# Second-layer products moved behind the branches of a mixture-of-experts kernel, with two loads and two gathers in another order

## The chip, the cores and the metric

The kernel runs on one core of one Trainium2 chip. The metric is the time of one execution on the device, in microseconds (us). It has five engines that matter here: TensorE (PE, with PEld for its weight loads and a sequencer that reads its instructions), VectorE (DVE), ScalarE (ACT), GpSimd (POOL) and SyncE (SP).

## What is computed

Attention within chunks of 64 positions, and then a layer of eight experts of which each row takes one:

```python
def _attn_ref(q, k, v) -> np.ndarray:
    ...
    scores = scale * np.matmul(q_c, k_c.transpose(0, 1, 2, 4, 3))
    scores = scores - np.max(scores, axis=-1, keepdims=True)
    attn = np.exp(scores)
    attn = attn / (np.sum(attn, axis=-1, keepdims=True) + 1e-09)
    out = np.matmul(attn, v_c)
...
    logits = x @ w_gate
    expert_idx = np.argmax(logits, axis=1)
...
    for e in range(E):
        mask = expert_idx == e
        ...
        xe = x[mask]
        h = np.maximum(xe @ w1[e], 0.0)
        ye = h @ w2[e]
        out[mask] = gate_w[mask, None] * ye
```

There are 4608 rows of 512 numbers, each expert's first layer is 512 x 1024 and its second 1024 x 512, all in float32.

## The kernel before, in words

**Slots.** The first 120 us or so compute attention and the gate and sort the rows by expert in DRAM. The rest, which the change touches, runs in slots: one slot is 256 rows of one expert and, where that saves a slot of its own, 64, 128 or 192 extra rows of the same expert. How many extra rows a slot has is known only on the device (`kind`: 0, 1, 2, 3), so each slot has four forms behind branches (L1323 to L1325): `form_a` without extra rows, and `form_x` with 64, 128 or 192. Behind the branches comes the common part of the slot, and then the branch into the next slot's form. With these inputs slots 0 to 15 run, slot 0 still among the work on attention. Slot 1 has 64 extra rows, slots 5 and 7 as well, slot 9 and slot 12 have 192, slot 10 has 128, and the others none.

**Products.** Each float32 product is made of three products of split operands: high by high, low by high and high by low. The high part of weights and of hidden values is written by ScalarE (L82, L710), the low part by VectorE (L83, L715). A slot goes through eight blocks f of 128 hidden columns. For each, the first layer fills one bank (L683 in the plain form, L690 with extra rows), the ReLU writes high and low part, and two blocks later `block(f)` adds the second layer's products to bank U (rows 0 to 127, m = 0) and bank V (rows 128 to 255, m = 1), three matmuls each (L776 to L778). Extra rows have banks K and Q and go through `more(f)`.

**The end of a slot.** Before the change a form ends with blocks 4 and 5 for both banks, twelve products, and for extra rows with their finishes (L801 to L803, L807) and the stores of their results (L808; tile y2 for the first 128 or 64 extra rows, y3 for the next 64). The common part then splits the next rows (L663, L664; in slot 1 TensorE transposes them, L634), splits chunks 4 and 5 of the next weights (L82, L83), adds blocks 6 and 7 in bank U, and finishes bank U on ScalarE (L805). [...]

**Weights.** An expert's weights are sixteen chunks, high and low, for two sets in turn. They arrive in four raw tiles of two chunks each: raw0 for chunks 0 and 1, raw1 for 2 and 3, raw2 for 4 and 5, raw3 for 6 and 7. A split is one instruction on ScalarE and one on VectorE. `split_step(u, i)` splits one chunk behind block i and issues the load that can go as soon as a raw tile is free.

**Queues.** All indirect transfers go through GpSimd in the order of the code: the loads of weights (L581), the gathers of rows (L608: xg3 and xg5 for extra rows of the next slot, xg4 twice for the rows of the slot after it) and the stores (L808). Each counts on one of eight semaphores (DMASW0 to DMASW7), which the framework hands out in turn; in a form without a certain store an instruction on GpSimd adds what the store would have added. Who waits for a transfer in the common part waits for the semaphore's value there, and that includes every transfer counted on it before.

**Code.** `PLACE` and `addr_align` (in the 192-row form) set where the code of TensorE's forms stands in blocks of 256 instructions; `hint` tells TensorE's sequencer at block 4 which form comes next.

Of the kernel before, what the change touches and what calls it, by code (L numbers as in the profile page):

```python
# [40 lines left out]
XW = D + 16  # L41
HB = 3
WARM = 36
PLACE = {1: 87, 2: 110, 3: 110}
BLOCK = 256
SKEW = 128
BIG = 1.0e6
# [3 lines left out]
def attn_moe_kernel(ctx: ExitStack, tc: tile.TileContext, q, k, v, wg, w, w0, out):  # L51
# [27 lines left out]
    def split_chunk(par, c):  # L79
        hi, lo = w_hi[par][c], w_lo[par][c]  # L80
        src = raw[c // 2][:, (c % 2) * 1024:(c % 2 + 1) * 1024]
        nc.scalar.copy(hi, src)  # L82
        nc.vector.tensor_tensor(lo, src, hi.bitcast(F32), ALU.subtract)  # L83
# [20 lines left out]
    def bank(tag, shape):  # L104
        n = 1
        for x in shape[1:]:
            n *= x
        if tag == "S":
            t = psum[0].tile([P, 512], F32, name="psS", tag="S", bufs=2)
        else:  # L110
            t = slots[tag][turns[tag] % len(slots[tag])]
            turns[tag] += 1
        t = t[0:shape[0], 0:n]
        if len(shape) == 3:
            t = t.rearrange("p (a b) -> p a b", b=shape[2])
        return t
# [459 lines left out]
    def wset(u):  # L576

        return 0 if u < 2 else (u + 1) % 2

    def load_w(u, c):  # L580
        nc.gpsimd.indirect_dma_start(  # L581
            out=raw[c][:, :], out_offset=None,
            in_=w, in_offset=bass.IndirectOffsetOnAxis(ap=widx[:, u, c:c + 1], axis=0),
            bounds_check=4 * E * P - 1, oob_is_err=False)
# [21 lines left out]
    def rows_in(t, u, h):  # L606
        rows = TE[u] * P if u < 2 and h < 2 else NT
        return nc.gpsimd.indirect_dma_start(  # L608
            out=t[:, :], out_offset=None, in_=xd[0:rows, :],
            in_offset=bass.IndirectOffsetOnAxis(ap=place(u, h)[0:t.shape[0], :], axis=0),  # L610
            bounds_check=rows - 1, oob_is_err=False)
# [6 lines left out]
    def gather_x(u):  # L618
        rows_in(xg3, u, 2)
        rows_in(xg5, u, 3)  # L620
# [25 lines left out]
    def spread(u):  # L646

        for h in range(2):
            ids(u, rows_of(u)[h], h)
        for a in range(4):  # L650
            for b in range(4):
                nc.sync.dma_start(
                    xq.rearrange("p (h a) x -> p h a x", a=4)[b * 32:(b + 1) * 32, :, a, :],
                    xg4[a * 32:(a + 1) * 32, 2:4, b * P:(b + 1) * P])
# [63 lines left out]
    def gemm1(par, f, hh=None, hl=None):  # L718
        ph = bank("X", [P, BLK]) if f % 3 == 2 else bank("S", [P, BLK])
        gemm1_pe(par, f, ph)  # L720
        return gemm1_lo(ph, relu_hi(ph, hh), hl)
# [36 lines left out]
    def rest_0():  # L758

        gemm2(0, 7, h0[7], 1, last[0])  # L760
        finish(0, 1, last[0][1])
# [8 lines left out]
    def gemm2(par, f, h, m, py):  # L770
        gemm2_pe(par, f, *(x[:, m * P:(m + 1) * P] for x in h), py[m])
# [41 lines left out]
    def split_step(u, i):  # L813

        if i < 2:
            if u < 2:
                load_w(u + 1, 2 + i)
                return
            split_chunk(wset(u), 6 + i)
            if i == 1:  # L820
                load_w(u + 1, 3)
                load_w(u + 1, 2)
        else:
            split_chunk(wset(u + 1), i - 2)
            if i % 2:
                load_w(u + 2, i // 2 - 1)

    used = [0]

# [37 lines left out]
    def find_u(u):  # L867
        return find(idx[u % 3], rowm[:, u, :], rowm[:, u, :], KB - 1) if u < NU else iter(())
# [106 lines left out]
    def slot_kinds():  # L975

        S2 = [P, NU, E]
        for h in range(2):
            ids(1, rows_of(1)[h], h)
        yield "v"  # L980
        nc.vector.tensor_tensor(o_b, iota_f[:, 0:NU].unsqueeze(2).broadcast_to(S2),
                                end.broadcast_to(S2), ALU.is_equal)
        yield "v"
        nc.vector.tensor_tensor(o_b, o_b, knd.broadcast_to(S2), ALU.mult)
        yield "v"
        with nc.allow_low_precision("whole numbers"):
            nc.vector.tensor_reduce(kind[:, 0:NU], o_b, AX.X, ALU.add)
# [233 lines left out]
    h_of = h0[5:8] + h0[5:8] + [[hq.tile([P, BLK], F32R, name=f"{x}{f}") for x in ("hh", "hl")] for f in (6, 7)]  # L1221

    def rest(u, py):

        for f in (6, 7):
            gemm2(wset(u), f, h_of[f], 1, py)
        finish(u, 1, py[1])

    def slot(u, kd, nxt, left=None):
        par = wset(u)  # L1230
        py = [bank("UV"[m], [P, D]) for m in range(2)]
        if u > 1:
            spread(u + 1)

        def block(f, h, ms=(0, 1)):
            for m in ms:
                gemm2(par, f, h, m, py)

        def later():

            if u == 1:
                yield from slot_kinds()
                yield "v"
                yield from places()
            yield from find_u(u + 3)

        def some(x, n):
            for _ in range(n):
                next(x, None)

        def form_a():
            if u == 1:
                rest_0()
            if left is not None:
                rest(u - 1, left)
            h = []
            x = later()
            for f in range(8):
                h.append(gemm1(par, f, *h_of[f]))
                if f == 4 and u + 1 < SMAX:  # L1260

                    hint(u + 1, kind_of(u + 1, PE) if u == 1 else nxt)
                if f == 0 and u > 1:
                    gather_x(u + 1)
                if f == 5 and u > 1:
                    turn()
                    gather(u + 2)
                if f < 7:
                    if f < 6:
                        split_step(u, f)  # L1270
                    some(x, 5 if u == 1 else 1)
                if 1 < f < 6:
                    block(f - 2, h[f - 2])
            assert next(x, 0) == 0
            for f in (4, 5):
                block(f, h[f])

        def form_x(n):

            make_xt_x(u, n)  # L1280
            if u == 1:
                rest_0()
            if left is not None:
                rest(u - 1, left)
            pe = [bank(x, [P, D]) for x in ("K", "Q")[0:-(-n // EXT)]]

            h = []
            x = later()

            def more(f):  # L1290
                gemm2_x(par, f, h[f][1], pe)

            for f in range(8):
                h.append(gemm1_x(par, f, n, *h_of[f]))
                if f == 4 and u + 1 < SMAX:
                    hint(u + 1, kind_of(u + 1, PE) if u == 1 else nxt)
                if f == 0 and u > 1:
                    gather_x(u + 1)
                if f == 5 and u > 1:
                    turn()  # L1300
                    gather(u + 2)
                if f < 7:
                    if f < 6:
                        split_step(u, f)
                    some(x, 5 if u == 1 else 1)
                if 1 < f < 5:
                    block(f - 2, h[f - 2][0])
                if 1 < f < 7:
                    more(f - 2)
                if f == 4 and n > EXT:  # L1310
                    nc.tensor.addr_align(BLOCK, offset=PLACE[u if u == 1 else 3 if u >= SMIN - 1 else 2], max_nops=0)
            assert next(x, 0) == 0
            more(5)
            block(3, h[3][0])
            more(6)
            more(7)
            for f in (4, 5):
                block(f, h[f][0])
            for i, p in enumerate(pe):
                m = min(EXT, n - i * EXT)  # L1320
                finish(u, 2 + i, p, m)

        with tc.If(kd > 0, label=f"kind{u}") as c:  # L1323
            with tc.If(kd > 1, label=f"half{u}") as c2:
                with tc.If(kd < 3) as c3:  # L1325
                    form_x(EXT)
                with c3.Else():
                    form_x(EXW)
            with c2.Else():
                form_x(HALF)  # L1330
        with c.Else():
            form_a()

        nc.gpsimd.drain()
        if u == 1:
            make_xt(u + 1)
        else:
            make_xs()
        for c in (4, 5):
            split_chunk(wset(u + 1), c)  # L1340
        for f in (6, 7):
            block(f, h_of[f], (0,))
        finish(u, 0, py[0], on_act=True)
        if u + 1 < SMIN:
            return py
        rest(u, py)
# [54 lines left out]
```

## Time and profile before

| what | value |
|---|---|
| median of 3 runs | 570.3 us (568.74 to 572.33) |
| the profiled execution, its own time | 571.92 us |
| its span in the profile | 570.0 us, 13232 instructions |
| granted TensorE clock, mean | 0.994 of full speed |
| busy, TensorE / VectorE / ScalarE / GpSimd | 553.8 / 425.1 / 280.9 / 270.4 us |
| bytes moved | 102.70 MB, mean 180 GB/s |

A busy time is the sum of an engine's instructions, with overlaps counted once. TensorE's weight loads run beside its products. An instruction's start and duration are on the clock of the span, which begins at 0; 570.0 of the 571.92 us lie inside it. [...]

### The profile page before, as it was taken

The numbers are of one execution on the slowest core, as the hardware profiler recorded it, in microseconds if no ns is written. First come the engines' busy times: TensorE is split into PE (matmuls) and PEld (weight loads), VectorE is DVE, ScalarE is ACT, GpSimd is POOL, SyncE is SP. The second block draws the span as 40 slices with busy tenths as digits, with TensorE's granted clock in tenths as the row PEclk, the third lists the DMA queues.
The fourth block names the chain that finished last, engine by engine and source line by source line (L and its number), as shares of the span: only waits on it lengthen the run. The fifth ranks groups of instructions, "written<-read, shape, count | busy, mean of one in ns | idle before, by whom it ended". The sixth has DMA issues, their size and how long they took to land.

```text
span 570.0 us, 13232 instructions
## 1 busy us (share of the span) xinstructions
PE 553.8 (97%) x4858; PEld 488.3 (86%) x4858; DVE 425.1 (75%) x832; ACT 280.9 (49%) x542; POOL 270.4 (47%) x289
## 2 busy tenths in 40 slices
PE   5999999999999999999999999999998999999995
PEld 5888888888998888989898898888988888798894
DVE  8889999996694978776787588645666764588775
ACT  1477776662244464554555355424444542456453
POOL 6013763586643754535484575522514242275352
PEclk9899999999999999999999999999999999999998
DMA  8999999744674652456145636554622662232121
GB/s 273 399 326 347 376 340 361 269 157 184 231 257 138 185 184 61 137 188 218 44 139 174 210 93 208 163 189 147 209 72 85 205 206 67 68 104 77 22 59 39
DMA packets 49038, 102.70 MB, mean 180 GB/s; under 512 B 14176, under 2 KB 28512, under 8 KB 45312
## 3 DMA queue, kind: packets, MB, share of 16 engines
q0 software_dynamic: 19776, 61.14, 31.4%
q1 hardware_dynamic: 29120, 39.88, 21.1%
q8 instruction: 63, 1.03, 0.7%
q14 instruction: 79, 0.65, 0.4%
HBM read 113.75 MB, written 19.56 MB: 234 GB/s over the span
## 4 chain that ended last, share of the span: by engine, by line
PE 76%; issue 10%; DMA 5%; POOL 3%; DVE 2%; POOLq 1%; ACT 1%; ACTq 0%
PE psS L683 12%; PE psS L690 10%; PE psS L251 6%; DMA xg<-xd,idx 5%; PE psV L776 4%; PE psV L777 4%; PE psV L778 4%; PE psU L778 4%; PE psU L777 4%; PE psU L776 4%; PE psL L690 3%; PE psL L683 3%; PE psU L306 3%; PE psT L329 2%; PE psT L297 2%
## 5 line engine op out<-in xcount | busy, mean ns | idle before, releaser
L83 DVE TENSOR_TENSOR wlo<-raw,whi 128x1024 fp32r<-128x1024 f32 x118 | 142.3, 1216 | 16.9 <-ACT whi L82 16.3
L82 ACT CAST whi<-raw 128x1024 fp32r<-128x1024 f32 x118 | 121.9, 1046 | 2.2 <-DMA raw<-in_w,widx 2.2
L581 POOL DMA_INDIRECT raw<-in_w,widx x62 | 71.9, 1160 | 91.1 <-DVE wlo L83 62.2
L710 ACT ACTIVATE hh<-psS 128x256 fp32r<-128x256 f32 x98 | 37.7, 385 | 156.8 <-PE psS L683 79.5
L808 POOL DMA_INDIRECT out_y<-y,oid x40 | 51.9, 1299 | 110.4 <-issue 35.3
L683 PE MATMUL psS<-xhl,whi 128*128 128x256 f32 x496 | 91.8, 284 | 0.9 <-PE psV L778 0.5
L608 POOL DMA_INDIRECT xg<-xd,idx x68 | 78.7, 1157 | 26.5 <-issue 17.3
L683 PEld LDWEIGHTS psS<-xhl,whi 128*128 128x128 f32 x496 | 79.7, 191 | 5.4 <-issue 1.3
L715 DVE SCALAR_TENSOR_TENSOR hl<-psS,hh 128x256 fp32r<-128x256 f32 x98 | 41.1, 421 | 57.1 <-ACT xx L694 37.8
L683 PE MATMUL psS<-xhl,wlo 128*128 128x256 f32 x248 | 70.2, 283 | 0.0
L690 PE MATMUL psS<-xhl,whi 128*128 128x320 f32 (+2 forms) x288 | 59.8, 333 | 0.5 <-ACT xhl L674 0.5
L690 PEld LDWEIGHTS psS<-xhl,whi 128*128 128x128 f32 x288 | 49.6, 188 | 4.6 <-ACT xhl L674 0.6
L776 PE MATMUL psV<-whi,hh 128*128 128x512 f32 x128 | 51.1, 399 | 1.5 <-issue 1.5
L776 PE MATMUL psU<-whi,hh 128*128 128x512 f32 x128 | 50.4, 394 | 0.0
L777 PE MATMUL psU<-wlo,hh 128*128 128x512 f32 x128 | 50.4, 393 | 0.0
L778 PE MATMUL psU<-whi,hl 128*128 128x512 f32 x128 | 50.2, 392 | 0.0
L777 PE MATMUL psV<-wlo,hh 128*128 128x512 f32 x128 | 50.1, 391 | 0.0
L778 PE MATMUL psV<-whi,hl 128*128 128x512 f32 x128 | 50.0, 390 | 0.0
L683 PEld LDWEIGHTS psS<-xhl,wlo 128*128 128x128 f32 x248 | 47.4, 191 | 0.0
L90 POOL TENSOR_TENSOR wlo<-raw,whi 128x512 fp32r<-128x512 f32 x16 | 20.2, 1277 | 43.7 <-DMA kb<-in_k 27.3
L452 POOL DMA_INDIRECT xd<-xb,di x32 | 31.7, 989 | 18.0 <-issue 13.1
L776 PEld LDWEIGHTS psV<-whi,hh 128*128 128x128 f32 x128 | 24.0, 188 | 7.7 <-issue 2.3
(255 smaller groups left out, 1150.1 us busy)
## 6 DMA issues: line engine op xcount, KB each, us to landing
qt<-in_q SPq DMA_DIRECT2D x17, 512.0 KB
xg<-xg SPq DMA_DIRECT2D x224, 32.0 KB
vb<-in_v SPq DMA_DIRECT2D x12, 512.0 KB
kb<-in_k SPq DMA_DIRECT2D x22, 256.0 KB
raw<-in_w SPq DMA_DIRECT2D x16, 256.0 KB
spare<-in_k SPq DMA_DIRECT2D x12, 256.0 KB
spare<-in_v SPq DMA_DIRECT2D x6, 512.0 KB
xg<-xd,idx POOLq DMA_INDIRECT x68, 3.5
```

What stands on the lines that cost most here:

```text
L82: nc.scalar.copy(hi, src)
L83: nc.vector.tensor_tensor(lo, src, hi.bitcast(F32), ALU.subtract)
L581: nc.gpsimd.indirect_dma_start(out=raw[c][:, :], out_offset=None, in_=w, in_offset=bass.IndirectOffsetOnAxis(ap=widx[:, u, c:c + 1], axis= ...
L608: return nc.gpsimd.indirect_dma_start(out=t[:, :], out_offset=None, in_=xd[0:rows, :], in_offset=bass.IndirectOffsetOnAxis(ap=place(u, h)[ ...
L683: nc.tensor.matmul(ph, a, b[:, kc, 0:BLK], start=kc + i == 0, stop=kc + i == 5)
L690: nc.tensor.matmul(ph, a[par][kc][:, f * 128:(f + 1) * 128], b[:, kc, 0:BLK + n], start=kc + i == 0, stop=kc + i == 5)
L710: nc.scalar.activation(hh, ph, AF.Relu)
L715: nc.vector.scalar_tensor_tensor(hl, ph, 0.0, hh.bitcast(F32), ALU.max, ALU.subtract)
L776: nc.tensor.matmul(py, hh, wh, start=f == 0, stop=False)
L777: nc.tensor.matmul(py, hh, wl, start=False, stop=False)
L778: nc.tensor.matmul(py, hl, wh, start=False, stop=f == 7)
L808: nc.gpsimd.indirect_dma_start(out=outs[m], out_offset=bass.IndirectOffsetOnAxis(ap=oid[u % 3][0:n, m:m + 1], axis=0), in_=y, in_offset=No ...
```

## The change

Three edits, in every slot:

1. A form ends with block 4 in bank U alone. Block 4 in bank V and block 5 in both, nine products, move behind the branch into the common part, ahead of blocks 6 and 7. The code of the forms becomes shorter, and the constants of `PLACE` grow by 36.
2. `split_step` issues the load of raw2 before that of raw3.
3. The gathers for extra rows (`gather_x`) move from behind block 0 to behind the load of raw0 in the fourth `split_step`.

```diff
-PLACE = {1: 87, 2: 110, 3: 110}
+PLACE = {1: 123, 2: 146, 3: 146}
...
             if i == 1:
+                load_w(u + 1, 2)
                 load_w(u + 1, 3)
-                load_w(u + 1, 2)
         else:
             split_chunk(wset(u + 1), i - 2)
             if i % 2:
                 load_w(u + 2, i // 2 - 1)
+                if i == 3 and u > 1:
+                    gather_x(u + 1)
...
-                if f == 0 and u > 1:
-                    gather_x(u + 1)
...
-            for f in (4, 5):
-                block(f, h[f])
+            block(4, h[4], (0,))
...
-                if f == 0 and u > 1:
-                    gather_x(u + 1)
...
-            for f in (4, 5):
-                block(f, h[f][0])
+            block(4, h[4][0], (0,))
...
         for c in (4, 5):
             split_chunk(wset(u + 1), c)
+        block(4, h_of[4], (1,))
+        block(5, h_of[5])
         for f in (6, 7):
             block(f, h_of[f], (0,))
```

What that does to the engines' orders. TensorE, end of the 128-row form, before (bank U and V for block 4 with hh_2680, then for block 5 with hh_2714, then the jump to the common part):

```order
L776 MATMUL psU_88<-whi1_6_2749,hh_2680 128x512
L777 MATMUL psU_88<-wlo1_6_2757,hh_2680 128x512
L778 MATMUL psU_88<-whi1_6_2749,hl_2685 128x512
L776 MATMUL psV_89<-whi1_6_2749,hh_2680 128x512
L777 MATMUL psV_89<-wlo1_6_2757,hh_2680 128x512
L778 MATMUL psV_89<-whi1_6_2749,hl_2685 128x512
L776 MATMUL psU_88<-whi1_6_2749,hh_2714 128x512
...
L778 MATMUL psV_89<-whi1_6_2749,hl_2792 128x512
L1325 UNCONDITIONAL_BRANCH
```

and the same place now, with the last of the extra rows' products (bank K) ahead of it:

```order
L778 MATMUL psK_93<-whi1_7_2750,xx_4321 128x512
L776 MATMUL psU_88<-whi1_6_2749,hh_2680 128x512
L777 MATMUL psU_88<-wlo1_6_2757,hh_2680 128x512
L778 MATMUL psU_88<-whi1_6_2749,hl_2685 128x512
L1321 UNCONDITIONAL_BRANCH
```

The nine products between the fourth and the jump are gone from here; they follow in the common part, so that on the way through a slot their order is the old one. Only in slot 1 do the transposes of L634 come before them.

GpSimd, the part of one slot from the first extra gather to the last weight load, before (xg_65 and xg_66 are the two extra gathers, raw_2742 is raw3, raw_2741 raw2, raw_67 raw0, raw_68 raw1; ISA is the instruction that adds to a semaphore):

```order
L608 DMA xg_65<-xd,idx_285 128x528
L1397 ISA
L608 DMA xg_66<-xd,idx_285 64x528
L581 DMA raw_2742<-in_w,widx 128x2048
L581 DMA raw_2741<-in_w,widx 128x2048
L581 DMA raw_67<-in_w,widx 128x2048
L590 COMPARE_AND_BRANCH
L590 UNCONDITIONAL_BRANCH x2
L608 DMA xg_64<-xd,idx_286 128x528 x2
L581 DMA raw_68<-in_w,widx 128x2048
```

and now:

```order
L581 DMA raw_2741<-in_w,widx 128x2048
L1395 ISA
L581 DMA raw_2742<-in_w,widx 128x2048
L581 DMA raw_67<-in_w,widx 128x2048
L608 DMA xg_65<-xd,idx_285 128x528
L608 DMA xg_66<-xd,idx_285 64x528
L590 COMPARE_AND_BRANCH
L590 UNCONDITIONAL_BRANCH x2
L608 DMA xg_64<-xd,idx_286 128x528 x2
L581 DMA raw_68<-in_w,widx 128x2048
```

Raw2 has gone from the fourth place to the first, and the two extra gathers from the head of the row to behind raw0. As the semaphores are handed out in this order, others share one now.

ScalarE, common part of the same slot, before, with the semaphores that an instruction waits for:

```order
L663 CAST xhl<-y_2762 128x2x256 [waits DVE_49,PE_49]
L663 CAST xhl<-y_2762 128x2x256 [waits PE_49]
L82 CAST whi_4_73<-raw_2741 128x1024 [waits DMASW7_49]
L82 CAST whi_5_74<-raw_2741 128x1024
L805 ACTIVATE y_2762<-psU,gate_106 128x512 [waits DMASW2_49,DVE_49,PE_49]
```

and now:

```order
L663 CAST xhl<-y_2762 128x2x256 [waits DVE_49,PE_49]
L663 CAST xhl<-y_2762 128x2x256 [waits PE_49]
L82 CAST whi_4_73<-raw_2741 128x1024 [waits DMASW4_49]
L82 CAST whi_5_74<-raw_2741 128x1024
L805 ACTIVATE y_2762<-psU,gate_106 128x512 [waits DMASW2_49,DVE_49,PE_49]
```

The instructions stand as before. The split of chunk 4 waits for DMASW4 instead of DMASW7, to a value that counts raw2 and, behind it, the store of y2 at the end of the same slot's form; DMASW7 counted raw2 alone at that place.

## Rows read from the trace of the kernel before

**Rows 1.** The page, busy time of TensorE (us, share of the span, instructions).

```profile
PE 553.8 (97%) x4858; PEld 488.3 (86%) x4858; DVE 425.1 (75%) x832; ACT 280.9 (49%) x542; POOL 270.4 (47%) x289
```

**Rows 2.** Waits of TensorE, 250 to 570 us: total, times, longest.

```profile
PE psV L776 <- issue: 1.5, 1, 1.5
PE psS L683 <- PE psV L778: 0.5, 1, 0.5
```

**Rows 3.** Branches of TensorE's sequencer: ns min/median/max, start; slots 10, 10, 12, 7.

```profile
L1325 PEldq COMPARE_BRANCH  x1: 3282/3282/3282, 422.5 to 422.5; - x1
...
L1323 PEldq COMPARE_BRANCH  x1: 3208/3208/3208, 426.3 to 426.3; - x1
...
L1325 PEldq COMPARE_BRANCH  x1: 3613/3613/3613, 488.4 to 488.4; - x1
...
L1324 PEldq COMPARE_BRANCH  x1: 326/326/326, 324.6 to 324.6; - x1
```

**Rows 4.** Timeline, end of slot 10: start us, us, engine, instruction, [idle before].

```profile
421.53 0.28 DVE L697 SCALAR_TENSOR_TENSOR xx<-psS,xx 128x128 fp32r<-128x128 f32 x1
...
422.48 0.39 PE L776 MATMUL psK<-whi,xx 128*128 128x512 f32 x1
...
426.56 0.39 PE L776 MATMUL psU<-whi,hh 128*128 128x512 f32 x1
...
429.55 0.50 PE L776 MATMUL psV<-whi,hh 128*128 128x512 f32 x1 [1.46 <-issue]
```

**Rows 5.** Timeline of TensorE, end of slot 12 and start of slot 13.

```profile
488.39 0.39 PE L796 MATMUL psQ<-whi,xx 128*128 128x512 f32 x1
...
495.89 0.36 PE L683 MATMUL psS<-xhl,whi 128*128 128x256 f32 x1 [0.51 <-PE psV L778]
```

**Rows 6.** The chain of waits, 386 to 398 us, slots 9 to 10: start, us, what.

```profile
390.22 3.67 DMA out_y<-y,oid
...
396.14 1.93 PE psS L690 x11
```

**Rows 7.** Timeline of ScalarE, end of slot 9.

```profile
391.18 2.00 ACT L82 CAST whi<-raw 128x1024 fp32r<-128x1024 f32 x2
393.74 0.69 ACT L805 ACTIVATE y<-psU,gate 128x512 f32<-128x512 f32 x1 [0.56 <-PE psU L778]
394.83 0.59 ACT L674 CAST xhl<-psT 128x512 fp32r<-128x512 f32 x1 [0.40 <-PE psT L672]
```

**Rows 8.** Timeline of GpSimd, VectorE and TensorE, slots 7 to 8.

```profile
328.26 4.02 POOL L808 DMA_INDIRECT out_y<-y,oid  x1 [3.82 <-DVE y L803]
...
329.11 2.34 DVE L83 TENSOR_TENSOR wlo<-raw,whi 128x1024 fp32r<-128x1024 f32 x2
...
333.24 0.75 DVE L807 TENSOR_SCALAR y<-psV,gate 128x512 f32<-128x512 f32 x1 [1.52 <-PE psS L683]
333.91 0.41 DVE L715 SCALAR_TENSOR_TENSOR hl<-psS,hh 128x256 fp32r<-128x256 f32 x1
...
336.20 0.39 PE L778 MATMUL psU<-whi,hl 128*128 128x512 f32 x1
```

**Rows 9.** DMA queues, 332.7 to 333.3 us: packets, MB, share.

```profile
q0 software_dynamic: 48, 0.02, 14.6%
```

**Rows 10.** Timeline of VectorE and GpSimd in slot 7, a split beside a weight load.

```profile
316.81 1.23 DVE L83 TENSOR_TENSOR wlo<-raw,whi 128x1024 fp32r<-128x1024 f32 x1 [0.38 <-ACT whi L82]
316.92 1.98 POOL L581 DMA_INDIRECT raw<-in_w,widx  x1 [0.31 <-issue]
```

**Rows 11.** Timeline, slot 8's first extra gather, and its first use in slot 9.

```profile
338.65 1.56 POOL L608 DMA_INDIRECT xg<-xd,idx  x1 [0.30 <-issue]
...
352.56 0.51 PE L672 MATMUL psT<-ident,xg 128*128 128x128 f32 x3
```

**Rows 12.** Timeline, end of slot 1: VectorE and TensorE.

```profile
176.27 0.68 DVE L802 TENSOR_TENSOR y<-psK,y 64x512 f32<-64x512 f32 x1 [2.29 <-ACT y L801]
...
176.60 0.39 PE L778 MATMUL psV<-whi,hl 128*128 128x512 f32 x1
```

## The prediction

> **What bounds the kernel now.** I read the page's busy times first, then what TensorE waits for in the slots, then the branches of its sequencer, then the two ends of slots at which something is late, and last GpSimd beside VectorE.
>
> TensorE is busy for 553.8 of 570.0 us [rows 1]. From 250 us on its waits are single: 1.5 us for "issue" at L776 in bank V and 0.5 us at L683, each once [rows 2], and two smaller ones at extra rows' transposes and their first products. So whatever hides beside TensorE is free, and a change that keeps its products can win only those few us; it can lose more wherever an operand comes late.
>
> Both waits of rows 2 are jumps. The compare-and-branch that ends the 128-row form of slot 10 holds the sequencer 3.28 us from 422.5, and the next one, from the common part into the plain form, 3.21 us from 426.3 [rows 3]. At the end of the 192-row form of slot 12 it is 3.61 us; the 64-row form's jump takes 0.33 us. What the sequencer has already passed on keeps TensorE going meanwhile: the jump at 422.5 begins with the product at 422.48, and the first product behind it starts at 426.56 [rows 4], which at one product per 0.227 us is 18 products of cover, 4.1 us. One long jump fits under that. Two in a row don't: six products stand between them, and TensorE waits 1.46 us at 429.55.
>
> **The change part by part.** The order of the products on TensorE stays as it is in all slots but the first, so their time drops out. Four things are left.
>
> *The jump comes nine products earlier.* It is followed by 15 products instead of six before the next jump. In slot 10 the sequencer would reach it at 422.5 - 9 x 0.227 = 420.5, but the last extra product needs VectorE's low half, which ends at 421.53 + 0.28 = 421.81 [rows 4], so about 421.9. With 3.28 us it resumes at 425.2. What was passed on ends where product 4 of bank U ends, at 422.48 + 9 x 0.227 = 424.5: a new gap of 0.7 us there. The next jump is met after 15 products' issue, about 0.75 us later at 425.9, takes 3.2 us and lets bank V's products through at 429.0 instead of 429.55. So -0.6 us; between 0 (the new gap eats it) and -1.46 (both hidden). In slot 12 the jump moves from 488.4, by the same rule, to about 486.7 and ends at 490.3, just before the nine remaining products of cover run out at 488.39 + 9 x 0.23 = 490.46 [rows 5]; the second jump then lies under 21 products, and the first product of slot 13, at 495.89, loses its wait and a little issue: -0.66, between +0.4 and -0.7. In slot 9, whose end shows no wait for a jump, I take 0. The plain and 64-row forms have short jumps: 0.
>
> *A wait on another transfer.* Software transfers count on eight semaphores in turn. Before, the first gather for extra rows shared its semaphore with the store of the extra results (tile y2) that stands at the form's end; the next slot's transposes therefore waited for that store too. Now the load of weight chunk 4 and 5 (tile raw2) stands first in GpSimd's row and takes that place, so ScalarE's split of chunk 4 in the common part waits for y2's landing although its own data came long before. Behind it on ScalarE stand the second split, the finish of bank U (L805), the extra rows' copy (L674) and the next slot's first ReLU; behind those, VectorE and TensorE.
>
> From slot 9 to 10 the store lands at 390.22 + 3.67 = 393.89, where the two splits had begun at 391.18 [rows 6, 7]. Then 2.00 for the splits, 0.69 for the finish and 0.59 for the copy give 397.2, and TensorE wants that copy at 396.14: +1.1 us (between 0, if ScalarE's pair was late for another reason, and +1.5). From 10 to 11 and from 12 to 13 TensorE stands at the next form's jump or has two more microseconds in hand: 0.
>
> After the 64-row slots 5 and 7 it depends on when the store starts to move. In slot 7 it is issued at 328.26 and takes 4.02 us on GpSimd [rows 8]; its 48 packets run only at 332.7 to 333.3 [rows 9], just behind the 4.02 us. If that time stays, the splits start at 333.3, the pair ends at 335.3, VectorE's pair 1.2 us behind it (2.34 for two) at 336.6, then four tiny instructions, the finish of bank V (0.75) and the low half (0.41): 338.0, and TensorE wants that low half at 336.20: +1.75, twice. But GpSimd's 4.02 us looks like VectorE's doing: a weight load issued 0.11 us after a split began on VectorE took 1.98 us and ended at 318.90, which is 0.86 us after that split's end [rows 10], and 328.26 + 4.02 = 332.28 is 0.83 us after the end of the pair at 329.11 + 2.34 = 331.45. With ScalarE held, VectorE's pair is held too; the store's issue then ends 0.85 us after L664, near 330.0, its landing comes at 331.0 and the low half at 335.9, 0.3 us before it is wanted. I take 0 for both slots, since the lag of rows 10 repeats so closely, and keep +1.75 each as the upper end.
>
> [...]
>
> *Loads and gathers trade places on GpSimd.* Eight transfers are issued in a slot as before. The gathers for extra rows now come behind three loads, which wait for splits, some 8 us later by my estimate: in slot 8 the first was issued at 338.65 and its rows are wanted at 352.56 [rows 11], so 6 us are left where a store with its landing takes 3.67 [rows 6], and 0 is its price. What hides it is the rest of the slot; issued 2 us later still, it would cost what it is late. The two row gathers and raw1 behind them keep their place from the fourth split on, at most some 2.6 us later when GpSimd is busy, with over 6 us of cover. Raw2 comes earlier, which TensorE doesn't notice: 0.
>
> *Slot 1.* There the transposes of the next rows (L634) now come before the nine products, and must wait until the extra rows' banks are read out, which VectorE's instruction at 176.27 ends at 176.95. TensorE would be at the second four at about 176.6, where bank V's last product 4 stood [rows 12]: +0.35, of which a later stall of 0.2 gives some back; I take +0.2.
>
> The constants that place the code rise by 36 each, as the code in front of them shrinks, so that the forms keep their places: 0 (a long jump gone or added, 3.3 us under 4 us of cover, at the outside +1).
>
> Sum: -0.6 - 0.66 + 1.1 + 0 + 0.2 = about 0. Made against the profiled execution (571.92 us, span 570.0), that is 572.0. It lies 1.6 above the median of the runs, 570.3, so against that the forecast is 570.5 us. About 1%, 5.7 us, is what a measurement of this kernel can tell from no change.
>
> **The rivals.**
>
> *Gains only.* Every added wait is hidden and the pair of jumps closes fully: -1.46 - 0.7 = -2.2, 568.2. For it: rows 2 hold just these waits. Against it: the sum for 9 to 10, where nothing is left to hide 2.7 us of delay on ScalarE.
>
> *The late store reaches TensorE.* The time on GpSimd stays 4.02 us in slots 5 and 7 and the delay on ScalarE is not caught up: +1.75 twice and +1.1 is +4.6, less 1.2 won, 573.7. Slower by over 1% it becomes when the lag runs through the slot: held up by some 4, 4 and 3 us at the three places, all of it on TensorE, it is +11, less the 1.2: 580. It decides from the point at which the low half of a slot's first block comes more than the 1.9 us late that lie between the end of that low half, 333.91 + 0.41, and 336.20 [rows 8]. For it: one semaphore surely counts both. Against it: what rows 10 show, and a lag that VectorE's idle time between blocks makes good.
>
> *The cover isn't 18 products.* If the sequencer runs ahead as far as it likes, the jump's place matters little. [...] As a mechanism here: with deeper cover the jump at 422.5 would have been met earlier already, so moving it would bring nothing and the nine products less of cover behind it cost 0.7 to 1.4 in slots 10 and 12, giving 573.5 with the wait of slot 9.
>
> *No visible effect for another reason.* TensorE's order is the same, so if the semaphore's wait falls early too, everything is 0: 570.3. It is part of the forecast's case.
>
> **How the numbers follow.** Chances: the forecast (all between -1.5 and +1.5) 0.55; gains only 0.13; the late store at +3.5 0.17, and beyond +5.7 0.06; the cover 0.09. The range reaches from 567.2 (all gains, and the scatter of the median, which the runs from 568.74 to 572.33 show to be over 1 us) to 574.8 (both 64-row slots paid, and the same scatter). Faster by over 1%: 0.03, as no rows hold 5.7 us to win. Slower by over 1%: 0.07, the second rival's far end and a little. Within 1%: 0.90.
>
> **What would show it right or wrong.** Right: the branch at the end of slot 10's form begins near 421.9 less whatever came before, and the wait of 1.46 us at L776 shrinks to under a microsecond, partly as a new one at bank V's product 4; the wait at L683 behind slot 12 goes; at the start of slot 10 L690 waits about a microsecond for ScalarE's L674, and ScalarE's L82 before it names a store as what it waited for. GpSimd's L808 in slots 5 and 7 falls from 4.02 to about 2 us. Wrong: L808 stays at 4 us and L778 in the first block of slots 6 and 8 waits over a microsecond for VectorE; extra rows' transposes wait for a gather; or a jump of 3 us appears at a 64-row or plain form.

## The result, and the profile after

The changed kernel takes 577.18 us (median of 6 runs, 574.23 to 578.62) against 570.69 us (6 runs) for the kernel before: ratio 1.0108, 95% interval 1.0074 to 1.0143. It is slower by 1.1%. The forecast, 570.5 us and hardly a change, was wrong, and so was its range, which ended at 574.8.

The profiled execution of the changed kernel took 576.67 us, its span is 574.8. Where the 4.8 us of span lie can be read by the starts of the same product in both timelines (after minus before). The attention ahead of the slots differs from one execution to the next (slot 1 starts between 2.7 us earlier and 1.6 us later than before in the profiles of the other kernels below), so only the steps from one line to the next count:

| place | product | after minus before | step |
|---|---|---|---|
| slot 1 | products to 172 us | -2.0 | |
| slot 2 | products at 195 us | -1.8 | +0.2 |
| slot 6 | first L683 behind block 0, 285.01 in before | -0.95 | +0.85 |
| slot 8 | products at 345 us | +3.5 | +4.45 |
| slot 10 | products at 405 us | +5.05 | +1.55 |
| slot 11 | products at 435 us | +4.15 | -0.9 |
| slot 13 | L683, 495.89 in before | +3.67 | -0.5 (0.65 won at this product, 0.17 lost ahead of it) |
| end | last product | +3.7 | 0 |
| end of the span | behind the last product | +4.8 | +1.1 |

So in the slots 5.7 us are lost, and 1.1 behind them: 6.8, about as much as the medians differ (6.5). The waits of TensorE from 250 us on, the answer to [rows 2], name the places (same view and columns):

```profile
PE psU L778 <- DVE hl L715: 3.4, 2, 2.8
PE psS L690 <- ACT xhl L674: 2.3, 2, 1.9
PE psV L776 <- issue: 0.6, 1, 0.6
```

The 1.5 us at L776 of [rows 2] have shrunk to 0.6 and the 0.5 at L683 is gone, as forecast. In their place TensorE waits 3.4 us for the low half of a slot's first block and 2.3 for extra rows. Busy times say nothing of this: TensorE stands at 97% in both pages [rows 1]. One line of ScalarE's waits points to the cause, which the experiments then test:

```profile
ACT whi L82 <- DMA out_y<-y,oid: 18.5, 5, 4.5
```

Five times, once in each slot with extra rows from slot 5 on, ScalarE's split of the weights waits for a store of results, up to 4.5 us. Before slot 8, for one, the load of raw2 itself had been issued at 307.5, and the store only at 327.30. The same place in the page, the group of L82:

```profile
L82 ACT CAST whi<-raw 128x1024 fp32r<-128x1024 f32 x118 | 122.0, 1046 | 18.5 <-DMA out_y<-y,oid 18.5
```

**Slots 7 to 8**, answering to [rows 8] (timeline of GpSimd, ScalarE, VectorE and TensorE):

```profile
327.30 1.75 POOL L808 DMA_INDIRECT out_y<-y,oid  x1 [3.84 <-DVE y L803]
...
331.30 2.00 ACT L82 CAST whi<-raw 128x1024 fp32r<-128x1024 f32 x2 [4.47 <-DMA out_y<-y,oid]
...
332.38 2.36 DVE L83 TENSOR_TENSOR wlo<-raw,whi 128x1024 fp32r<-128x1024 f32 x2 [4.16 <-ACT whi L82]
...
337.05 0.75 DVE L807 TENSOR_SCALAR y<-psV,gate 128x512 f32<-128x512 f32 x1 [2.04 <-issue]
337.71 0.41 DVE L715 SCALAR_TENSOR_TENSOR hl<-psS,hh 128x256 fp32r<-128x256 f32 x1
...
338.18 0.80 PE L778 MATMUL psU<-whi,hl 128*128 128x512 f32 x1 [2.77 <-DVE hl L715]
338.78 0.63 PE L776 MATMUL psV<-whi,hh 128*128 128x512 f32 x1
```

The store's issue takes 1.75 us instead of 4.02, as the lag of [rows 10] had let expect. Yet ScalarE starts only 4.0 us after the issue began, where the forecast had put some 2.7. The store's packets had run by then. Of 48, the view of the DMA queues (packets, MB, share) has 47 from 329.5 to 330.3 and one from 330.3 to 331.3, and none of this queue's from 330.4 on; so nearly a microsecond lies between their end and ScalarE's start at 331.30:

```profile
q0 software_dynamic: 47, 0.02, 11.8%
...
q0 software_dynamic: 1, 0.00, 0.1%
```

VectorE's pair ends at 334.74 and its four tiny instructions at 335.0, but the finish of bank V, which stands with that bank's blocks 6 and 7 at the head of the next form, begins at 337.05, 2.04 us idle "for issue". VectorE's sequencer shows where the time lies; its rows are a compare-and-branch into the plain form and the semaphore instruction that is the first thing behind it:

```profile
L1319 DVEq COMPARE_BRANCH  x1: 56/56/56, 333.9 to 333.9; - x1
...
L807 DVEq EVENT_SEMAPHORE  x1: 50/50/50, 336.9 to 336.9; - x1
```

The branch itself lasts 56 ns, but the row behind it comes 3.0 us later. The run with a hint, below, tests whether this gap goes when VectorE's sequencer is told of the next form. Before, the same two rows stood at 330.3 and 333.1, a gap of 2.8 us, and it lay in time in which VectorE waited for TensorE's product anyway (1.52 us, put down to L683 in [rows 8]):

```profile
L1323 DVEq COMPARE_BRANCH  x1: 56/56/56, 330.3 to 330.3; - x1
...
L807 DVEq EVENT_SEMAPHORE  x1: 50/50/50, 333.1 to 333.1; - x1
```

Behind TensorE's 2.77 us the products come every 0.42 us (338.78, 339.20, 339.63) instead of every 0.23 (342.06, 342.29, 342.52). Busy times by stretch show the granted clock (start:end, length, busy time and count of PE, PEld, DVE, ACT and POOL, then PEclk, DMA share, GB/s):

```profile
338.18:341.30 3.12, 3.12 (x10) 2.73 (x11) 3.12 (x5) 0.00 (x0) 2.10 (x2) 0.50 0.24 84
341.30:345.00 3.70, 3.70 (x27) 3.46 (x26) 3.58 (x7) 1.32 (x2) 1.01 (x1) 0.99 0.04 5
```

For 3.1 us the granted clock is 0.50, and behind it 0.99. My estimate from these rows is about 1.5 us lost on top of the wait, half of the 3.12.

**Slots 5 to 6**: the same kind of store and the same wait of ScalarE. But here VectorE's branch is followed within 0.5 us (280.86 to 281.38), its finish of bank V starts at once behind the tiny instructions, and TensorE waits only 0.58:

```profile
274.36 1.74 POOL L808 DMA_INDIRECT out_y<-y,oid  x1 [3.83 <-DVE y L803]
...
278.29 2.00 ACT L82 CAST whi<-raw 128x1024 fp32r<-128x1024 f32 x2 [4.40 <-DMA out_y<-y,oid]
...
281.91 0.75 DVE L807 TENSOR_SCALAR y<-psV,gate 128x512 f32<-128x512 f32 x1
...
283.04 0.50 PE L778 MATMUL psU<-whi,hl 128*128 128x512 f32 x1 [0.58 <-DVE hl L715]
```

**Slots 9 to 10**, answering to [rows 6, 7] (L674 copies out the transposes of slot 10's extra rows, L672; the first line is the same product in the kernel before):

```profile
395.97 0.87 PE L690 MATMUL psS<-xhl,whi 128*128 128x384 f32 x4
```

```profile
397.72 1.99 ACT L82 CAST whi<-raw 128x1024 fp32r<-128x1024 f32 x2 [2.95 <-DMA out_y<-y,oid]
399.74 0.69 ACT L805 ACTIVATE y<-psU,gate 128x512 f32<-128x512 f32 x1
400.32 0.58 ACT L674 CAST xhl<-psT 128x512 fp32r<-128x512 f32 x1
...
400.95 0.97 PE L690 MATMUL psS<-xhl,whi 128*128 128x384 f32 x4 [1.88 <-ACT xhl L674]
```

**The jumps** of slots 10 and 12, answering to [rows 3] (branches of TensorE's sequencer stand under PEldq):

```profile
L1321 PEldq COMPARE_BRANCH  x1: 3343/3343/3343, 426.9 to 426.9; - x1
...
L1319 PEldq COMPARE_BRANCH  x1: 2519/2519/2519, 430.8 to 430.8; - x1
...
L1321 PEldq COMPARE_BRANCH  x1: 3861/3861/3861, 490.8 to 490.8; - x1
```

**The end of the kernel.** On GpSimd a DRAIN instruction stands ahead of the last stores (L1334 before, L1330 after); it takes 2.8 us before and 5.2 after:

```profile
L1334 POOLq DRAIN  x1: 2781/2781/2781, 558.2 to 558.2; - x1
```

```profile
L1330 POOLq DRAIN  x1: 5151/5151/5151, 561.9 to 561.9; - x1
...
566.12 0.69 ACT L805 ACTIVATE y<-psU,gate 128x512 f32<-128x512 f32 x1 [0.80 <-PE psU L778]
...
567.92 1.02 POOL L808 DMA_INDIRECT out_y<-y,oid  x1 [3.43 <-issue]
569.25 1.00 POOL L808 DMA_INDIRECT out_y<-y,oid  x1 [0.31 <-issue]
```

Before, the drain ended at 560.9, 2 us before ScalarE had bank U's results for the store. Now it ends at 567.0, and those results lie ready since 566.81; the store goes out at 567.92, and the last one starts 1.8 us behind the last product's end instead of 1.1. That is 0.7 of the 1.1 us; the rest lies behind the last store, 5.5 us from its issue to the end of the span instead of 5.2, and what it comes from isn't shown.

### The profile page after: what moved, and what is told of

It reads as the page before. It is cut to its first block, busy times and chain, and to the rows that moved or that the text cites. A ratio compares the mean times of both kernels' runs of the same rounds, so it can differ in the third digit from the quotient of the medians.

```text
span 574.8 us, 13239 instructions
## 1 busy us (share of the span) xinstructions
PE 555.3 (97%) x4858; PEld 489.3 (85%) x4858; DVE 423.0 (74%) x832; ACT 280.7 (49%) x542; POOL 262.6 (46%) x289
## 4 chain that ended last, share of the span: by engine, by line
DMA 35%; PE 26%; issue 24%; POOL 11%; POOLq 2%; ACT 1%; DVE 1%; SPq 0%; ACTq 0%
DMA xg<-xd,idx 34%; POOL raw L581 6%; PE psS L251 6%; POOL xg L608 4%; PE psU L306 3%; PE psS L683 2%; PE psT L329 2%; PE psL L341 2%; PE psT L297 2%; PE psQ L329 2%; PE psS L690 1%; PE psQ L297 1%; PE psL L1042 1%; DMA kb<-in_k 1%; POOLq L1330 1%
## 5 line engine op out<-in xcount | busy, mean ns | idle before, releaser
L82 ACT CAST whi<-raw 128x1024 fp32r<-128x1024 f32 x118 | 122.0, 1046 | 18.5 <-DMA out_y<-y,oid 18.5
L581 POOL DMA_INDIRECT raw<-in_w,widx x62 | 69.9, 1127 | 102.0 <-DVE wlo L83 50.3
L808 POOL DMA_INDIRECT out_y<-y,oid x40 | 50.0, 1251 | 115.9 <-issue 25.7
L683 PE MATMUL psS<-xhl,whi 128*128 128x256 f32 x496 | 92.2, 285 | 0.4 <-ACT at L298 0.4
L608 POOL DMA_INDIRECT xg<-xd,idx x68 | 74.8, 1099 | 24.4 <-issue 18.6
L683 PEld LDWEIGHTS psS<-xhl,whi 128*128 128x128 f32 x496 | 80.5, 193 | 4.6 <-ACT at L298 0.7
L683 PE MATMUL psS<-xhl,wlo 128*128 128x256 f32 x248 | 70.5, 284 | 0.0
L690 PE MATMUL psS<-xhl,whi 128*128 128x320 f32 (+2 forms) x288 | 60.0, 333 | 2.3 <-ACT xhl L674 2.3
L690 PEld LDWEIGHTS psS<-xhl,whi 128*128 128x128 f32 x288 | 49.5, 188 | 6.9 <-ACT xhl L674 2.9
L776 PE MATMUL psV<-whi,hh 128*128 128x512 f32 x128 | 51.6, 403 | 0.6 <-issue 0.6
L776 PE MATMUL psU<-whi,hh 128*128 128x512 f32 x128 | 50.3, 393 | 0.0
L683 PEld LDWEIGHTS psS<-xhl,wlo 128*128 128x128 f32 x248 | 47.7, 192 | 0.0
L778 PEld LDWEIGHTS psU<-whi,hl 128*128 128x128 f32 x128 | 24.2, 189 | 9.7 <-DVE hl L715 4.6
```

What stands on the lines that cost most here:

```text
L581: nc.gpsimd.indirect_dma_start(out=raw[c][:, :], out_offset=None, in_=w, in_offset=bass.IndirectOffsetOnAxis(ap=widx[:, u, c:c + 1], axis= ...
L608: return nc.gpsimd.indirect_dma_start(out=t[:, :], out_offset=None, in_=xd[0:rows, :], in_offset=bass.IndirectOffsetOnAxis(ap=place(u, h)[ ...
L683: nc.tensor.matmul(ph, a, b[:, kc, 0:BLK], start=kc + i == 0, stop=kc + i == 5)
L690: nc.tensor.matmul(ph, a[par][kc][:, f * 128:(f + 1) * 128], b[:, kc, 0:BLK + n], start=kc + i == 0, stop=kc + i == 5)
L776: nc.tensor.matmul(py, hh, wh, start=f == 0, stop=False)
L778: nc.tensor.matmul(py, hl, wh, start=False, stop=f == 7)
```

## The experiments

Theory A: ScalarE's split waits for a store that shares a semaphore with raw2, which is the doing of edits 2 and 3 together; edit 1 wins a little. Rival B: the moved products cost the time. Rival C: what is issued later on GpSimd costs it, not the semaphore. Theory D and rival E, on the largest step, stand at the run with the hint. All ratios are to the kernel before on the same chip, with 95% intervals.

**Edit 1 alone** (e1_products): the diff above without the lines on `load_w` and `gather_x`.

> Edit 1 alone (nine products and the code constants), GpSimd's order as before. Theory A (the shared semaphore costs the time, the moved products win a little): slots 10 and 12 win 0.7 each, slot 1 loses 0.2, so 1.2 us below the kernel before, ratio 0.998; no wait of L778 for hl over 0.5 us, ScalarE's L82 waits for no store. Rival B (the moved products cost it, by jumps with less cover behind them): 5 to 6 us above the kernel before, ratio 1.010.

Measured: 0.9972 (0.9943 to 1.0, so no change is just within it). In the profile the slots win 0.9 us. TensorE's waits from 250 us on:

```profile
PE psV L776 <- issue: 0.8, 1, 0.8
PE psT L672 <- DMA out_y<-y,oid: 0.6, 1, 0.6
PE psS L690 <- ACT xhl L674: 0.5, 1, 0.5
```

No wait for a low half, and none of ScalarE for a store. B falls.

**Edits 2 and 3 alone** (e2_queue):

```diff
-                load_w(u + 1, 3)
                 load_w(u + 1, 2)
+                load_w(u + 1, 3)
...
                 load_w(u + 2, i // 2 - 1)
+                if i == 3 and u > 1:
+                    gather_x(u + 1)
...
-                if f == 0 and u > 1:
-                    gather_x(u + 1)
```

> Edits 2 and 3 alone (GpSimd's order), the products at the forms' ends as before. Theory A: the losses of the changed kernel without its gains: 0.8 after slot 5, 4.4 after slot 7, 1.6 after slot 9 and 1.1 at the end, 7.9 us above the kernel before, ratio 1.014; ScalarE's L82 waits about 4.4 us for the store out_y after slots 5 and 7. Rival B: no more than 1 us from the kernel before.

Measured: 1.0131 (1.0085 to 1.0178). The changed kernel's losses without the gains of edit 1:

```profile
PE psU L778 <- DVE hl L715: 3.3, 2, 2.8
PE psS L690 <- ACT xhl L674: 2.5, 2, 2.0
PE psV L776 <- issue: 1.7, 1, 1.7
```

In the slots the profile of this run loses 10.0 us, more than the 6.6 of edits 2 and 3 in the changed kernel (5.7 and the 0.9 that edit 1 wins in its profile). The clock stayed low longer, 0.50 from 339.9 to 346 and again behind the 2.0 us at L690. The profiled execution (582.77 us) is one of the longest of the six; by the medians the run is 7.1 us above the kernel before, near the 7.9 expected.

**Edits 1 and 3** (e3_edits13): the changed kernel with raw3 loaded ahead of raw2 again.

```diff
-                load_w(u + 1, 2)
                 load_w(u + 1, 3)
+                load_w(u + 1, 2)
```

> Edits 1 and 3: as the changed kernel, but raw3 is loaded ahead of raw2, so that raw3 shares its semaphore with the store of y2 and raw2 with that of y3, which only slots 9 and 12 have. Theory A: no wait of ScalarE's L82 for a store after slots 5 and 7, a longer one after slot 9 (2 to 2.5 us at TensorE), 1.1 at the end: about 2.4 us above the kernel before, ratio 1.004. Rival C (the later gathers and what they push behind them cost it, not the semaphore): 5 to 6 us above, as the changed kernel.

Measured: 1.0062 (1.0024 to 1.01), 0.2% over what A expected; the upper end of the interval still reaches C's 5 to 6 us, so the trace has to decide. GpSimd issues the gathers as late as in the changed kernel, and only two loads have changed places. The waits for a low half are gone; after slots 9 and 12 raw2 now waits for the later of the two stores:

```profile
PE psS L690 <- ACT xhl L674: 3.0, 2, 2.5
PE psV L776 <- issue: 1.0, 1, 1.0
...
ACT whi L82 <- DMA out_y<-y,oid: 7.4, 3, 3.7
```

So which transfer shares with which store decides, and not how late GpSimd issues. C falls for the slots. This run also bears out how [rows 10] were read: with ScalarE on time in slot 7, VectorE's pair of splits is early again, and the store's issue is back at its old length:

```profile
329.88 4.02 POOL L808 DMA_INDIRECT out_y<-y,oid  x1 [3.84 <-DVE y L803]
```

**Edits 1 and 2** (e4_edits12): the gathers stay behind block 0.

> Edits 1 and 2: the extra gathers stay behind block 0, raw2 is loaded ahead of raw3. Raw2 shares its semaphore with a later transfer only. Theory A: as edit 1 alone, 1.2 us below the kernel before, ratio 0.998, and the last store not later than in it. If the swap of the loads were what costs: several us above.

Measured: 0.9961 (0.9924 to 0.9999). The swap of the loads alone costs nothing, since raw2 then stands third. In this run and in edit 1 alone the last store starts 1.07 us behind the last product, as in the kernel before; in the three runs with the gathers moved as in edit 3 (the changed kernel, edits 2 and 3, edits 1 and 3) it is 1.7 to 1.8, and in the run with the hint, next, 1.5. The later last store belongs to edit 3.

**The hint for VectorE** (e6_hint): the changed kernel, with VectorE's sequencer told of the next form too.

```diff
-            tc.mark_branch_hint_location(f"half{u}", hint=0, engines=PE)
+            tc.mark_branch_hint_location(f"half{u}", hint=0, engines=PE if u < 3 else PE + [mybir.EngineType.DVE])
...
-            tc.mark_branch_hint_location(f"kind{u}", hint=(kd + 3) >> 2, engines=PE)
+            tc.mark_branch_hint_location(f"kind{u}", hint=(kd + 3) >> 2, engines=PE if u < 3 else PE + [mybir.EngineType.DVE])
```

> The changed kernel, with the hint on the next slot's form given to VectorE's sequencer too (so far to TensorE's alone), from slot 3 on. Theory D: of the 4.4 us lost after slot 7, 0.9 is the late weights; 2.0 is VectorE's jump into the plain form, which begins 3.6 us later than before and whose code arrives 3.0 us after the jump, in front of the finish of bank V; and 1.5 is the granted clock of 0.50 that follows TensorE's 2.8 us of waiting. With the hint the code is there: TensorE's wait for hl at L778 in slot 8 falls from 2.8 to about 0.8 us, the clock stays at 1.0, and the kernel is 3 to 3.5 us faster than the changed one, ratio to the kernel before about 1.005. Rival E: the late finish waits for something else, and ratio and wait stay, 1.011 and 2.8 us.

Measured: 1.0046 (1.002 to 1.0072). VectorE's branch and finish in slot 8, TensorE's wait there, and the granted clock behind it:

```profile
L1319 DVEq COMPARE_BRANCH  x1: 81/81/81, 333.3 to 333.3; - x1
...
L807 DVEq EVENT_SEMAPHORE  x1: 50/50/50, 333.8 to 333.8; - x1
...
331.77 2.36 DVE L83 TENSOR_TENSOR wlo<-raw,whi 128x1024 fp32r<-128x1024 f32 x2 [4.14 <-ACT whi L82]
...
334.31 0.75 DVE L807 TENSOR_SCALAR y<-psV,gate 128x512 f32<-128x512 f32 x1
...
335.44 0.50 PE L778 MATMUL psU<-whi,hl 128*128 128x512 f32 x1 [0.63 <-DVE hl L715]
...
336.20:339.30 3.10, 3.10 (x20) 2.76 (x20) 3.10 (x7) 2.04 (x3) 2.79 (x2) 1.00 0.30 110
```

The weights are as late as without the hint, but the row behind the branch comes after 0.5 us instead of 3.0, the finish follows the tiny instructions at once, TensorE waits 0.63 us, and the granted clock stays at 1.00. Theory D holds as far as the times go, and rival E falls: of the 4.45 us after slot 7, 0.9 remain, so the gap behind VectorE's jump and the lower clock behind it are some 3.5. What the sequencer does in the gap isn't shown. The two went together, so no run shows the share of each.

**Edits 1 and 2 with that hint** (e9_hint12), and **edits 1 and 2 again** (e10_edits12) on the same chip:

> Edits 1 and 2 with the hint for VectorE as well, the control for the run with the hint: without late weights VectorE's jumps lie under TensorE's work. Theory D: no gain from the hint, the time of edits 1 and 2 alone within 1 us, ratio to the kernel before 0.995 to 0.999. Rival: the hint itself saves some 3 us in any kernel, ratio about 0.991.

> Edits 1 and 2 once more, for the comparison with the hint on the same chip: 0.4 to 2 us below the kernel before, ratio 0.996 to 0.999.

Measured: 0.9983 (0.9934 to 1.0033) with the hint, 0.9952 (0.9912 to 0.9992) without it. The medians are 1.4 us apart, a little more than the 1 us expected, with overlapping intervals, and the rival's 0.991 lies outside. So the hint wins nothing where the weights come on time: in the trace of edits 1 and 2 (e4_edits12) VectorE's finish at L807 waits for "issue" once, 0.5 us, and TensorE for no low half. Its 3.5 us in the run before are those of the late jump, with the clock behind it.

**Another order of the gathers** (e7_gathers), on edit 1:

```diff
                 load_w(u + 1, 3)
+                rows_in(xg5, u + 1, 3)
                 load_w(u + 1, 2)
...
                 load_w(u + 2, i // 2 - 1)
+                if i == 3 and u > 1:
+                    rows_in(xg3, u + 1, 2)
...
-                if f == 0 and u > 1:
-                    gather_x(u + 1)
```

> Edit 1, and another order on GpSimd: raw3, the gather of xg5, raw2, raw0, the gather of xg3, the two of xg4, raw1. Raw3 now shares its semaphore with y2's store and xg5 with y3's; raw2 and xg3 share with nothing that is late. Theory A: TensorE's wait of 0.6 us at L672 and that of 0.5 at L690 at the start of slot 10, which edit 1 alone still has, go as well; ScalarE's L82 waits for no store; the end loses up to 0.5 us to the later gather. 1.5 to 2.3 us below the kernel before, ratio 0.996 to 0.997. If the sharing isn't the cause, the two waits stay and the time is that of edit 1 alone or above.

Measured: 1.0001 (0.9968 to 1.0034), a miss in the time. TensorE's wait at L672 is gone as expected, that of 0.5 at L690 is not:

```profile
PE psV L776 <- issue: 0.8, 1, 0.8
PE psS L690 <- ACT xhl L674: 0.5, 1, 0.5
```

In the slots the profile of this run is 0.4 us better than that of edit 1 alone (-1.25 against -0.88 from 155 us to the last product, relative to before). It gives back more at the end, where one gather behind the fourth split is enough to make the last store late: it starts 1.77 us behind the last product, and the span ends 7.1 us behind it instead of 6.2. So the half microsecond at L690 is no wait for the store, which I had taken it for.

**The code constants** (e8_place), on edit 1:

```diff
-PLACE = {1: 123, 2: 146, 3: 146}
+PLACE = {1: 87, 2: 110, 3: 110}
```

> Edit 1 with the code constants of before (87, 110, 110), so that the forms stand 36 instructions earlier in their blocks. Forecast's term: 0 to 1 us against edit 1 alone (a long jump more, under cover). Rival: the constants carry the gain, and one or more jumps of 3 us come into the open, 2 to 6 us above edit 1 alone.

Measured: 0.9994 (0.9955 to 1.0033), 0.2% above edit 1 alone, with overlapping intervals, so the times alone don't shut out the rival's lower end. In the trace no branch of TensorE makes it wait more than 0.1 us longer than in edit 1 alone from 250 us on. One wait appears in its trace that the kernel before and edit 1 alone don't have, early in slot 1:

```profile
154.95 0.45 PE L690 MATMUL psS<-xhl,wlo 128*128 128x320 f32 x2 [1.51 <-issue]
```

That is 1.5 us of the profile; the forecast's "at the outside +1" was a little short. The wait lies between two products of one group, with no branch of TensorE's sequencer there, so it isn't the long jump that the forecast named, and its cause isn't shown.

## Why the prediction was wrong

*Jumps (-0.6 and -0.66).* Right, step by step. In the changed kernel products are 5.05 us later there than before, so the forecast's 421.9 for the jump is 426.9, where it stands; the new gap of 0.7 us in front of bank V's block 4 measures 0.58; the step in the table is -0.9 instead of -0.6, as the second jump took 2.5 us instead of 3.2. In slot 12 the jump begins at 490.8 (486.7 + 4.15), and the wait of 0.51 is gone. Edit 1 alone shows the gain by itself: 0.9 us in the profile, 0.9972 in the runs, though the interval of the runs just reaches 1.0. The rival of a deeper cover falls with it, since it had these gains at nothing.

*Slot 1 (+0.2).* Right: +0.2. *The code constants (0):* no loss shows as they were changed; if they hadn't been, 1.5 us of the profile.

*Slot 9 to 10 (+1.1).* Right in kind, half a microsecond short: 1.55. The store took 4.0 us from its issue to ScalarE's start (393.71 to 397.72 in the trace), where I had put 3.67, from a wait of TensorE for the same store. And TensorE's first product on the copy stood at 395.97 before, not at the 396.14 that I had read from the chain of waits. The rest follows as told, L674 at 400.32 and TensorE behind it.

*The 64-row slots (0, with +1.75 each as upper end).* This is the step that failed, in three places. First, "its landing comes at 331.0": the store's issue did get short, as the lag of [rows 10] let expect, so that part of the argument was right. But from the beginning of the issue to ScalarE's start it was 3.9 and 4.0 us in the two slots, not the 2.7 (328.26 to 331.0) that I had taken from the end of its packets. The 3.67 us of [rows 6], which the forecast used for slot 9, already said so: with it the landing would have been at 331.9 and the low half 0.6 us late, and with 4.0 it is 1.0 late. How long the issue itself takes hardly counted: in the changed kernel ScalarE waits 3.6 to 4.0 us from the beginning of the issue at all five places, for issues of 1.02 to 1.75 us. The 0.3 us in hand became a wait of 0.58 in slot 6, a step of +0.85. Second, and the largest: I counted behind the split only the work of VectorE, "four tiny instructions, the finish of bank V (0.75) and the low half (0.41)". Between them stands a jump of VectorE, and the row behind it came 3.0 us later. It begins 1.5 us behind the start of the pair (332.38), where it began 1.2 us behind it before (329.11). With the pair 3.3 us later it moved 3.6 us (330.3 to 333.9) and came out from under the wait that used to cover it. Third, behind TensorE's wait of 2.77 us the granted clock fell to 0.50 for 3.1 us. Together +4.45 in slot 8, 2.5 times the upper end, which was itself built without jump and clock. With the hint the gap behind the jump is 0.5 us, the clock stays at 1.00, and 0.9 us remain, the size of slot 6.

*Loads and gathers (0).* Right for the slots: no transpose waited for a gather. Wrong at the end of the kernel, where I said nothing: +1.1, of which the later store is 0.7. "What hides it is the rest of the slot" holds while a slot follows. Behind the last one GpSimd's DRAIN ends later than the results are ready (567.0 against 566.81), and the two last stores follow it (567.92 and 569.25).

The sum with what was measured: +0.2 + 0.85 + 4.45 + 1.55 - 0.9 - 0.5 + 1.1 = 6.75, against 6.5 between the medians. The rival nearest to what came is the late store that reaches TensorE, with a chance of 0.23 in all. It has the right wait, but not for its reason: its condition, 4.02 us on GpSimd, didn't hold (1.75), and its far end was to come from a lag that runs through the slot. In fact the lag is made good within a slot, and most of the price came from the jump and the clock. Three readings of the forecast are off by 0.2 us without deciding anything: its terms add up to 0.04 us, which makes 570.3 of the runs and not 570.5; by its own steps the low half comes at 335.7 and not 335.9; and the 396.14 above.

What stays open: why the store in slot 7 lets ScalarE go only a microsecond after its last packets, what the 3.0 us behind VectorE's jump are, how the 3.5 us divide between jump and clock, and where 0.3 us behind the last store come from. And edits 1 and 2 against edit 1 alone lie within their intervals, so whether edit 2 is worth anything isn't told. By the ratios the best kernel of the study is edits 1 and 2: 0.9961 and 0.9952 in two comparisons.

## What to carry to other kernels

Where transfers count on a few semaphores in turn, changing their order changes who waits for whom: list for each wait all the transfers that its value counts, above all stores at the end of a branch. Then try the edits apart: here the kernel with all three is at 1.0108, with the loads in their old order at 1.0062, and with the gathers in their old place at 0.9961. When an instruction gets late, follow its engine's own queue to the next jump: here the gap of 2.8 us behind VectorE's jump lay under a wait in the kernel before, and the late splits pushed the jump out from under it, so that 2.04 us of 3.0 came into the open. And look at the last round by itself: here no transpose in the slots waited for a later gather, and the end of the kernel lost 1.1 us.

## What the runs showed of the hardware

The long jump of VectorE in slot 8 doesn't show in the branch's own row, which lasts 56 ns: its 3.0 us are only in the gap to the next row (0.5 us with the hint). TensorE's long branch at the end of slot 10 shows in its own row, 3.3 us.

An indirect store of results let its waiter go 3.6 to 4.0 us after the beginning of its issue at five places of the changed kernel, though the issues last between 1.02 and 1.75 us.

TensorE's granted clock fell to 0.50 behind waits of 2.77 us (changed kernel) and 2.83 us (edits 2 and 3), but the length of the wait alone doesn't tell: with edits 2 and 3 it was at 0.50 behind 2.02 us at L690 too, and with edits 1 and 3 it stayed at 1.00 behind 2.52 us at the same product.

```profile
404.21 1.65 PE L690 MATMUL psS<-xhl,whi 128*128 128x384 f32 x4 [2.02 <-ACT xhl L674]
```

```profile
399.71 0.96 PE L690 MATMUL psS<-xhl,whi 128*128 128x384 f32 x4 [2.52 <-ACT xhl L674]
```

The same four products take 1.65 us in the first and 0.96 in the second (the lines are from the timelines of edits 2 and 3, and of edits 1 and 3).
